# Batch 0's norm sums, the turn of v's second half and the first squares, reordered in the start-up of a fused attention and channel-mix kernel

## The chip, the core and the metric

One NeuronCore of a Trainium2 chip. The metric is the device time of one execution in microseconds (us). The engines are named as in the profile: PE (matmuls), PEld (its weight loads), DVE, ACT, POOL (which issues most input DMAs here) and SP.

## The reference, cut to what matters

```
qn = q / (norm(q over N) + 1e-6);  kn likewise                 # B, N, C = 4, 6208, 256
a  = softmax(kn^T qn)                                          # 256 x 256 for each batch
x  = v @ a                                                     # then the channel mix on x:
xk = mu_k * x + (1 - mu_k) * x_prev;  xr likewise with mu_r    # x_prev: the row before
y  = sigmoid(xr @ w_r) * (relu(xk @ w_k)**2 @ w_v)             # 256 -> 1024 -> 256
```

Batch 0's attention matrix must be complete before anything of the channel mix can start. After that the kernel walks over 48 blocks of 512 rows, with the sums of batches 1 to 3 interleaved.

## The kernel before

Batch 0 comes in groups of 512 rows (`DIRECT = NB - 1 = 11`). Each group is cast to bf16, squared for k's norms, and multiplied by PE. Squares of groups 1 to 10 are added on DVE; those of groups 0, 11, 12 and 13 go through PE as matmuls against a column of ones.

```python
    def group_cast(g, between):          # between: the two DVE steps of the sum of group g-1
        ...
        nc.vector.tensor_copy(row[...], f[0][:rows, :n]...)             # L145
        if g == NB - 1:
            v_mark()                     # a memset; it releases all of POOL's loads
        if between:
            between.pop(0)()             # L167
        mid = row[:rows, :n, P:P + C]
        if g < DIRECT:
            for go in between: go()      # L170, L172
            nc.scalar.copy(mid, f[1][:rows, :n])                        # L155
        else:
            nc.vector.tensor_copy(mid, f[1][:rows, :n])                 # L157
            for go in between: go()
        nc.scalar.activation(k2[:rows, :n], f[1][:rows, :n], AF.Square) # L160
```

After the sums, the softmax of batch 0 and the first block's x:

```python
    vT0 = const.tile([P, 2, M + 1], BF16, name="vT0")     # v of block 0, turned; 2 = halves of C
    ...
        def turn_half(a):      # PE: four 128x128 transposes into half a of ONE PSUM tile (L444)
        def take_half(a, copy):                            # that half to SBUF (L447)
            copy(vT0[:, :, a * H + 1:(a + 1) * H + 1]..., vT_ps[:, 2 * a:2 * a + 2])
        def difference(a):     # DVE: vT0 columns of half a minus the columns one to the left (L479)
        def product(a, ih):    # PE: four matmuls (L487) on vT0[:, ih, half a] and its difference
    ...
    evac_first()               # DVE: S out of PSUM, scaled (L332)
    turn_half(0)
    turn_half(1)
    take_half(1, nc.scalar.copy)
    turn()                     # PE: S transposed (L353)
    keep_warm(2)
    go = v_transpose_pe(1, nc.scalar.copy)                 # block 1's v, turned by PE (L425)
    invert_first(1)
    take_half(0, nc.vector.tensor_copy)
    difference(0)
    exp()                      # ACT (L361)
    go()
    weigh_first(0)             # DVE: a_sb (L373, L374)
    weigh_first(1)
    difference(1)
    for a in range(2):
        for ih in range(2):
            product(a, ih)
        for dh in range(2):
            mix_first("xk", a, dh)                         # DVE (L498)
```

Then `up_first` multiplies xk by w_k (L511), ACT applies Relu (L513, later L576), DVE squares (kk, L584). In the main loop, `square(0, 3)` (the first four kk of block 0) stood ahead of the two `mix` of block 1's xk (L556).

## Time and profile before

| | |
|---|---|
| time, first three runs | 505.04, 505.09, 505.9 us, median 505.09 |
| span of the profiled run | 503.7 us (that run took 505.44) |
| PE busy | 481.4 us, 96% |
| PE busy from 60 us on | 9.98 to 10.00 of every 10 us, but for 0.2 us near 130 and the last stretch |

Read the slices first: PE is full from the fourth slice on, so only the start-up can give anything. The prediction shows those lines and the waits.

### The profile page before, as it was taken

How to read it: one execution, taken by the hardware profiler on the slowest of the kernel's cores; microseconds unless marked ns; L12 is line 12 of the kernel's file. 1: busy time of each engine (PE TensorE's matmuls, PEld its weight loads, DVE VectorE, ACT ScalarE, POOL GpSimd, SP SyncE). 2: the span in 40 equal slices, each digit the busy share in tenths (PEclk: the TensorE clock that was granted, in tenths of full speed). 3: DMA queues.
4: the chain of work that ended last, by engine and by line, in shares of the span. 5: the costliest groups of instructions: out<-in, count | busy, mean ns of one | idle time of the engine just before them, and what ended most of it. 6: DMA issues, size and time to landing. Idle time of an engine off the chain costs nothing.

```text
span 503.7 us, 9289 instructions
## 1 busy us (share of the span) xinstructions
PE 481.4 (96%) x3429; PEld 330.8 (66%) x3429; DVE 429.0 (85%) x789; ACT 428.8 (85%) x872; POOL 97.3 (19%) x143
## 2 busy tenths in 40 slices
PE   1689999999999999999999999999999999999996
PEld 1355677667666666776676676666666666666675
DVE  2778899998988998899889899899888787878784
ACT  4788999899989989888999898988888878788784
POOL 0044332222233222122123322110031010000000
PEclk9999999999999999999999999999999999999999
DMA  8999999999999999996699999982295858343123
GB/s 324 419 311 192 183 143 188 142 183 199 210 216 196 217 177 179 146 208 110 142 195 146 181 184 185 163 145 73 64 208 97 160 88 151 80 103 89 55 72 105
DMA packets 131558, 83.46 MB, mean 166 GB/s; under 512 B 50548, under 2 KB 125624, under 8 KB 130488
## 3 DMA queue, kind: packets, MB, share of 16 engines
q0 software_dynamic: 55840, 33.01, 51.7%
q1 hardware_dynamic: 75352, 49.59, 42.9%
q8 instruction: 27, 0.44, 0.4%
q10 hardware_dynamic: 320, 0.26, 0.2%
q14 instruction: 19, 0.16, 0.1%
HBM read 78.71 MB, written 25.43 MB: 207 GB/s over the span
## 4 chain that ended last, share of the span: by engine, by line
PE 87%; DMA 6%; ACT 3%; DVE 2%; issue 1%; SPq 1%; ACTq 0%; DVEq 0%
PE vr_ps L603 32%; PE kT_ps L571 32%; PE vr_ps L599 8%; PE xT_ps L465 8%; PE s_ps L293 6%; DMA vT<-v_bf 3%; DMA f<-in_k_dram 3%; ACT k L160 1%; ACT qk L155 1%; SPq L125 1%; PE s_ps L199 0%; PE y_ps L643 0%; DVE xk L556 0%; PE st_ps L353 0%; DVE k L167 0%
## 5 line engine op out<-in xcount | busy, mean ns | idle before, releaser
L576 ACT ACTIVATE kr<-kT_ps 128x512 bf16<-128x512 f32 (+1 forms) x390 | 234.5, 604 | 32.9 <-PE kT_ps L571 29.0
L603 PE MATMUL vr_ps<-w_v_sb,kk 128*128 128x256 bf16 x1536 | 230.2, 273 | 0.0
L571 PE MATMUL kT_ps<-xk,w_k_sb 128*128 128x512 bf16 (+1 forms) x780 | 230.0, 377 | 0.2 <-DVE xk L556 0.2
L603 PEld LDWEIGHTS <-kk 128*128 128x128 bf16 x1536 | 150.3, 98 | 57.3
L584 DVE TENSOR_TENSOR kk<-kr 128x2048 bf16<-128x2048 bf16 (+1 forms) x148 | 125.8, 851 | 0.2 <-ACT kr L576 0.2
L613 DVE SCALAR_TENSOR_TENSOR res<-res,vr_ps 128x256 f32<-128x256 f32 x192 | 80.0, 417 | 50.9 <-ACT res L612 50.9
L571 PEld LDWEIGHTS <-w_k_sb 128*128 128x128 bf16 x780 | 75.5, 98 | 27.5 <-issue 0.6
L612 ACT ACTIVATE res<-vr_ps 128x256 f32<-128x256 f32 x192 | 76.5, 399 | 2.3 <-PE vr_ps L603 1.3
L599 PE MATMUL vr_ps<-w_r_sb,xr 128*128 128x256 bf16 x384 | 73.3, 273 | 0.0
L467 ACT CAST xT<-xT_ps 128x512 bf16<-128x512 f32 x94 | 55.9, 594 | 20.0 <-PE xT_ps L465 19.7
L556 DVE SCALAR_TENSOR_TENSOR xr<-delta,mu_t,xT 128x512 bf16<-128x512 bf16 x94 | 70.0, 746 | 0.0
L556 DVE SCALAR_TENSOR_TENSOR xk<-delta,mu_t,xT 128x512 bf16<-128x512 bf16 x94 | 70.0, 746 | 0.0
L599 PEld LDWEIGHTS <-xr 128*128 128x128 bf16 x384 | 37.6, 98 | 44.7 <-issue 0.4
L133 POOL DMA_DIRECT2D qk<-in_q_dram x39 | 26.1, 668 | 159.8 <-ACT kr L576 129.8
L465 PE MATMUL xT_ps<-vT,a_sb 128*128 128x512 bf16 x188 | 55.9, 379 | 0.2 <-DMA vT<-v_bf 0.2
L293 PE MATMUL s_ps<-qk 128*128 128x256 bf16 (+1 forms) x294 | 55.8, 273 | 0.0
L254 ACT ACTIVATE sq<-qk 128x1024 bf16<-128x1024 bf16 x48 | 51.1, 1064 | 0.0
L408 POOL DMA_DIRECT2D v_bf<-in_v_dram x47 | 35.7, 761 | 69.4 <-DMA vT<-v_bf 49.2
L199 PE MATMUL s_ps<-qk 128*128 128x384 bf16 (+2 forms) x98 | 19.1, 340 | 16.6 <-ACT qk L155 16.1
L546 DVE TENSOR_TENSOR delta<-xT 128x1024 bf16<-128x1024 bf16 x47 | 32.3, 686 | 1.1 <-ACT xT L467 1.1
L293 PEld LDWEIGHTS <-qk 128*128 128x128 bf16 (+1 forms) x294 | 28.5, 98 | 5.6 <-issue 0.8
L133 POOL DMA_DIRECT2D qk<-in_k_dram x39 | 25.9, 664 | 5.7 <-DMA v_bf<-in_v_dram 2.5
(114 smaller groups left out, 252.2 us busy)
## 6 DMA issues: line engine op xcount, KB each, us to landing
out_dram<-res SPq DMA_DIRECT2D x47, 512.0 KB, 4.9
v_bf<-in_v_dram POOLq DMA_DIRECT2D x47, 256.0 KB, 8.6
qk<-in_q_dram POOLq DMA_DIRECT2D x36, 256.0 KB, 8.4
qk<-in_k_dram POOLq DMA_DIRECT2D x36, 256.0 KB, 9.4
f<-in_q_dram SPq DMA_DIRECT2D x4, 1024.0 KB, 13.5
f<-in_k_dram SPq DMA_DIRECT2D x4, 1024.0 KB, 11.0
f<-in_q_dram SPq DMA_DIRECT2D x3, 512.0 KB, 7.7
f<-in_k_dram SPq DMA_DIRECT2D x3, 512.0 KB, 6.1
```

Source lines behind the costliest of these rows:

```text
L133: nc.gpsimd.dma_start(rows_at(qk, b, g, i)[:rows, :n], qk_src(t, b, g))
L293: nc.tensor.matmul(s_ps[:, ih, :], rows_at(qk, b, g, 0)[:rows, s, ih * P:(ih + 1) * P], rows_at(qk, b, g, 1)[:rows, s, :], start=t0 and ih ...
L465: nc.tensor.matmul(xT_ps, a_sb[:, b, ih, dh * P:(dh + 1) * P], vT[:, :, ih, :], start=ih == 0, stop=ih == 1)
L467: nc.scalar.copy(xT[:, dh, 1:], xT_ps)
L556: nc.vector.scalar_tensor_tensor(o[:, dh], st[i, "d"][:, dh], mu[:, dh:dh + 1], st[i, "x"][:, dh, :M], op0=OP.mult, op1=OP.add)
L571: nc.tensor.matmul(kT_ps[:, :m], w_k_sb[:, dh, fh * P:(fh + 1) * P], xk[:, dh, :m], start=dh == 0, stop=dh == 1)
L576: nc.scalar.activation(kr, kT_ps[:, :m], AF.Relu, scale=0.5 ** 0.5)
L584: nc.vector.tensor_tensor(st[i, "kk"][:, fh // 4 * 4 + lo:fh + 1, :m], kr, kr, op=OP.mult)
L599: nc.tensor.matmul(vr_ps[:, D:], xr[:, dh, s * P:(s + 1) * P], w_r_sb[:, dh, :], start=dh == 0, stop=dh == 1)
L603: nc.tensor.matmul(vr_ps[:, :D], kk[:, fh, s * P:(s + 1) * P], w_v_sb[:, fh, :], start=fh == 0, stop=fh == 7)
L612: nc.scalar.activation(res[:, s], vr_ps[:, D:], AF.Tanh, scale=0.5)
L613: nc.vector.scalar_tensor_tensor(res[:, s], res[:, s], 1.0, vr_ps[:, :D], op0=OP.add, op1=OP.mult)
```

## The change

Its intent: get batch 0's S to the softmax earlier, take v's half-copy off ACT's path to the exponential, and give PE block 1's xk before kk is squared. Three parts:

```diff
-    DIRECT = NB - 1
+    DIRECT = NB - 2                               # part 1: sums end with group 9
-        if g < DIRECT:
+        if g <= DIRECT:
-        for g in range(DIRECT + 1, LAST + 1):
+        for g in range(DIRECT + 2, LAST + 1):
         if g == DIRECT + 1:
             norms_first()                         # now ahead of group 11's matmuls
+        elif g == DIRECT + 2:
+            norms_of(g - 1)                       # eight more norm matmuls
     turn_half(0)
+    turn()                                        # part 2
     turn_half(1)
-    take_half(1, nc.scalar.copy)
-    turn()
...
     weigh_first(1)
+    take_half(1, nc.vector.tensor_copy)
     difference(1)
...
-            if j > 0 and 0 <= i + 1 < NBLK:
+            if j > 0 and 0 <= i + 1 < NBLK and (i, j) != (-1, 4):
                 square(i + 1, j - 1)              # part 3
...
                     mix(n, "xk", int(j > 4))
+                if (i, j) == (-1, 5):
+                    square(0, 3)
```

## The prediction

> **What bounds the kernel now.** I began with the page's totals and slices, for if TensorE (PE) is full, only stretches where it is not can be shortened.
>
> ```profile
> PE 481.4 (96%) x3429; PEld 330.8 (66%) x3429; DVE 429.0 (85%) x789; ACT 428.8 (85%) x872; POOL 97.3 (19%) x143
> PE   1689999999999999999999999999999999999996
> DMA  8999999999999999996699999982295858343123
> ```
>
> PE is 9 or more from the fourth slice (38 us) on; the busy time of each engine by stretches says how full that is (columns: window, length, then the busy us of PE, PEld, DVE, ACT, POOL):
>
> ```profile
> 20.00:40.00 20.00, 15.22 (x113) 9.06 (x112) 15.27 (x44) 16.67 (x26) 7.61 (x11) 1.00 1.01 320
> 40.00:60.00 20.00, 19.29 (x136) 12.51 (x137) 16.35 (x32) 18.73 (x39) 7.09 (x12) 1.00 1.24 202
> 60.00:70.00 10.00, 10.00 (x72) 6.78 (x71) 8.96 (x16) 9.21 (x20) 3.89 (x7) 1.00 1.39 144
> ```
>
> From about 50 us PE has no hole to remove. The change touches nothing after 50 us, so all it can do is start that stretch earlier; the end then moves by the same amount. What PE waited for in the whole run names the candidates (us in total, times, longest):
>
> ```profile
> PE s_ps L199 <- ACT qk L155: 16.1, 9, 10.1
> PE x_ps L487 <- DVE sm L373: 0.6, 1, 0.6
> PE s_ps L199 <- DVE qk L157: 0.6, 1, 0.6
> PE kT_ps L511 <- ACT kr L513: 0.3, 1, 0.3
> PE kT_ps L571 <- DVE xk L556: 0.2, 1, 0.2
> ```
>
> The 16.1 us is the loading of batch 0, which the change does not touch. The other four add up to 1.7 us: a ceiling of 0.3% of 505.09. The chain of waits (start, us, what) gives their order:
>
> ```profile
> 32.19 0.61 DVE qk L157
> 32.84 1.46 PE s_ps L199 x8
> ...
> 36.71 1.28 ACT L739
> 38.00 0.21 ACT gate L739
> 38.21 0.48 ACT vT L447
> 38.72 0.44 DVE vT L447
> 39.18 0.43 DVE delta L479
> ...
> 45.97 0.69 DVE delta L546
> 46.66 1.14 DVE kk L584
> 47.80 1.34 DVE xk L556 x2
> 49.17 0.38 PE kT_ps L571
> ```
>
> In this reading, group 11's cast (L157) holds S; v's half-copy on ACT holds the copy on DVE; kk stands ahead of the xk that PE needs.
>
> **What the Trainium skill says.**
> - "TensorE: Matmul & The Clock Gate", section "Wait — 56ns, not 53.3ns?": starts of small matmuls are never closer than about 25 ns. The trace agrees: the eight 128x1 norm matmuls start at 34.71 and the next matmul at 34.92, 26 ns each.
> - "ScalarE: Activation LUTs", section "What ACT_TABLE_LOAD costs": about 1283 ns. The load at 36.71 took 1.28 us. The page adds a drain of about 1380 ns; here the next ACT instruction starts at 38.00, so I do not charge it.
> - "PSUM — Partial Sum Buffer", section "PSUM bank collisions raise a hardware error": two engines may not touch one bank and quadrant together, so accesses are guarded by bank. This fits two waits: DVE's copy of v's first half at 38.72 behind ACT's copy of the second half (38.11, 0.57), both out of one bank; and the wait of PE L511 for ACT's Relu of the other half of its bank.
>
> **Part 1: group 10's sum.** Before, DVE halves group 10's squares while casting group 11. The first add (L167) waits for ACT's square to 31.77, and the cast L157 follows at 32.11. Its matmuls (L199 x8) start at 32.84, though the eight before them started at 30.82 and go one per 0.162 us: PE was free at 30.82+8x0.162 = 32.12. So 0.72 us is lost. After, the three DVE adds (0.42, 0.28, 0.42) are gone, the cast follows the memset at 31.69 and ends at about 32.3. PE first runs the norm matmuls, which need only group 9's sum (done 31.1) and group 10's square (31.7): 34.14 to 34.92 before, 0.78 us. So they take 32.12 to 32.90, and the group's matmuls start at 32.90, now behind PE alone. Added are eight norm matmuls for group 11, 0.21 us. Net: 0.78 has moved into the hole, 0.21 is new, and the start goes from 32.84 to 32.90, so the diagonal matmuls (L192, 35.57) come at 32.90+1.30+0.21+0.65 = 35.06: **0.51 us earlier**. The last group's inputs permit it: its k landed by 34.45, its square ends at 35.08, its norms are wanted at 35.53.
>
> **Part 2: v's second half.** The whole softmax chain moves by 0.51. The table load ends at 37.49, rk on DVE at 38.01 (38.52 before), the turned S at about 38.06. Moving the half-copy off ACT lets exp start near 38.1 instead of 38.61, only a little more than the shift itself. But DVE's first half-copy loses its wait: it starts at 38.05, not 38.72; then difference at 38.51, reciprocal 38.84, a_sb 39.03, and PE's product at 39.46 instead of 40.14: 0.68 gained. Block 1's v holds PE until 38.92 (its DMA) and its transposes issue until 39.36, so nearly nothing more was to be had. Turning the half behind S avoids meeting its DMA (PE waited until 37.20 for it, where S now wants to start at 37.23). The price: the half-copy (0.43, 0.46 start to start) now stands on DVE between a_sb and the second difference, which ends at 40.65 (40.87 before). The second product, which had slack there, now waits for it and starts its last matmul at 40.71+6x0.109 = 41.36 instead of 41.80. **0.44 remain.**
>
> **What cuts it.** PE's first up matmul (L511) waited for w_k's DMA:
>
> ```profile
> 41.99 0.10 PEld L511 LDWEIGHTS <-w_k_sb 128*128 128x128 bf16 x1 [0.20 <-DMA w_k_sb<-in_moe_w_k_dram]
> ```
>
> The memset that releases those loads stays at 31.63, so w_k lands at 42.0 as before. xk's first half is ready earlier, and both matmuls run at 42.08 and 42.19 instead of 42.08 and 42.47. Relu comes at 42.49 instead of 42.77, and the matmul behind it at 42.93 instead of 43.21. **About 0.3 of the 0.44 survives**, down to delta of block 1 at 45.67.
>
> **Part 3: kk behind xk.** Nothing is removed on DVE. Before, PE issued its first block-1 matmul at 48.63, would have been ready for the second 0.215 later at 48.85, and got xk at 49.17: 0.32 lost. xk now goes first and is done near 47.7, so **0.32 is added**. kk ends at 45.67+0.61+1.34+1.22 = 48.84; its first reader comes at 50.47-0.62 = 49.85, and the last kk (50.33-0.30 = 50.03) is read from 50.61. ACT's Relu of block 1 rewrites kr's buffer and so waits for kk: it could start at 49.1, after 48.84, so nothing is lost, with 0.2 us to spare.
>
> **Sum.** 0.51 grows to 0.68, falls to 0.44 and 0.30 on DVE and w_k's DMA, and gets 0.32 from the swap: 0.62 us. 505.09-0.62 = 504.5; span 503.7 to 503.1.
>
> **The rivals.**
> 1. The loads absorb part 1 and part 2 altogether: w_k lands some tenths later, or Relu's turn does not move. Then only the swap pays, 0.3 us: 504.8. For it: w_k is a wait of PE already, and the DMA rows are 9 throughout. Against: the loads' issue does not move, and PE was also held after w_k, by xk.
> 2. The swap backfires: kk, 1.34 us later in DVE's order, holds ACT's Relu of block 1, and through the three kT buffers PE. For it: ACT is 18.73 of 20 us busy there, margin 0.2 us. Against: kk's inputs are long ready. Cost up to 0.3: 504.8, and with rival 1 505.1.
> 3. The gain is lost in the long stretch: a transposing DMA issued at 113.25 landed 16.72 us later and held PE for 0.2 us. Other alignments could cost or save some tenths. PE's 10.00 of 10 us speaks against more.
> 4. w_k lands earlier, or xk's second half is later than worked out: the sum reaches 0.76 or 0.5.
>
> **Range and chances.** The mechanisms give 504.3 to 505.1. The three times before are 505.04, 505.09 and 505.9, so a median of a few runs may sit 0.2 off. I take 504.5, from 504.0 to 505.2. A change of 2% would be 10 us; the holes concerned hold 1.7. Faster 0.01, same 0.98, slower 0.01.
>
> **What would show it.** Right: PE's wait on L157 gone and L192 near 35.1; exp near 38.1; DVE's half-copy without a wait behind ACT; PE's product near 39.5, with a new wait of about 0.3 us before the second product; w_k still landing near 42.0; no wait on xk L556 near 48.6; the steady stretch 0.6 us earlier. Wrong: L192 late because group 11's cast or the last loads were the true bound; L511 as late as before (rival 1); ACT's L576 waiting for kk (rival 2); the start earlier but the end not (rival 3).

## The result

| | before | changed |
|---|---|---|
| median of 4 runs | 505.06 (505.03 to 505.9) | 504.73 (504.57 to 504.87) |
| ratio | | 0.9989, 95% interval 0.9972 to 1.0007 |
| span of the profiled run | 503.7 | 503.1 |

A ratio is the mean time of one kernel's runs over the mean of the other's runs of the same rounds, so not quite the ratio of the medians. The time lies in the predicted range, and the span is exactly the predicted 503.1. The steps under that number did not all come true: parts 1 and 3 gave what they were to give, and part 2, worked out as a small loss, took back most of part 1 (0.42 us alone, e2).

The changed kernel's page and its 40 to 60 us stretch (columns as in the prediction):

```profile
PE 482.3 (96%) x3437; PEld 331.2 (66%) x3437; DVE 429.7 (85%) x787; ACT 428.2 (85%) x871; POOL 96.9 (19%) x143
PE   2789999999999999999999999999999999999996
```

```profile
40.00:60.00 20.00, 19.42 (x139) 12.68 (x138) 16.78 (x31) 18.51 (x41) 7.07 (x12) 1.00 1.25 202
```

The eight new norm matmuls are there, and DVE has two instructions fewer (three adds gone, the half-copy come from ACT); of the 20 us, PE is busy 0.13 us more. What PE waited for in the whole run:

```profile
PE s_ps L199 <- ACT qk L155: 14.8, 7, 10.0
PE st_ps L353 <- DVE s_sb L332: 0.8, 1, 0.8
PE x_ps L487 <- DVE a_sb L374: 0.6, 1, 0.6
PE kT_ps L511 <- ACT kr L513: 0.3, 1, 0.3
PE x_ps L487 <- DVE vT L447: 0.2, 1, 0.2
```

Group 11's cast (L157) and block 1's xk (L556) are gone, as predicted. Two waits are new: of S's turn on DVE's s_sb (L353), since S no longer stands behind v's second half, and of the product on DVE's half-copy (vT L447). The chain of waits shows where it stands:

```profile
36.05 0.48 DVE rn L325
...
37.38 0.83 PE st_ps L353 x4
38.20 0.24 PE vT_ps L444 x4
38.47 0.44 DVE vT L447
38.93 0.43 DVE delta L479
...
40.28 0.34 DVE vT L447
40.66 0.50 PE x_ps L487 x3
41.19 0.38 ACT xT L491
```

Two things here are not in the prediction. PE's transposes of v's second half (L444), now behind S, stand ahead of DVE's copy of the *first* half. And the copy of the second half holds the *first* product. PE's instructions in order of time show the second point, in the kernel before and then in the changed one; the fourth and fifth matmul of the first product:

```profile
40.48 0.27 PE L487 MATMUL x_ps<-delta,a_sb 128*128 128x256 bf16 x1
40.59 0.28 PE L487 MATMUL x_ps<-vT,a_sb 128*128 128x256 bf16 x1
```

```profile
40.21 0.27 PE L487 MATMUL x_ps<-delta,a_sb 128*128 128x256 bf16 x1
40.66 0.27 PE L487 MATMUL x_ps<-vT,a_sb 128*128 128x256 bf16 x1 [0.18 <-DVE vT L447]
```

0.11 us from the fourth to the fifth became 0.45. A fair comparison needs a common zero, because group 10's matmuls start by chance at 30.82 in one profile and at 30.68 in the other (when the loads land). So from here positions count from the start of group 10's eight matmuls (L199 x8), the last work that no part touches:

| start, us after group 10 | before | changed |
|---|---|---|
| first product, 1st matmul | 9.32 | 9.19 |
| first product, 5th matmul | 9.77 | 9.98 |
| second product, last matmul | 10.98 | 11.18 |
| L511, the pair that waits for Relu | 12.39 | 12.59 |
| L465, x of block 2 | 18.57 | 18.44 |

At the pair, the changed kernel had *lost* 0.20 us; part 3 then gained 0.33. (0.30 of that loss belongs to neither part 1 nor part 2: one DVE instruction of 256 numbers, L325 at 36.05, took 0.47 us in this profile and 0.17 in the kernel before. The part on why the prediction was right comes back to it.) Of the 0.6 us between the spans, 0.27 were there at 49 us: 0.14 from the earlier group 10, minus 0.20, plus 0.33. The rest arose between 110 and 140 us. Matched by the starts of L465, the shift is 0.27 until 112, 0.44 at 120, 0.82 at 130, and 0.60 to 0.61 from 139 to the end. The kernel before had its 0.22 us wait on a transposing DMA there, which the changed one did not; its profiled run was also 0.38 us slower than its median. That the span came out at the predicted value was chance.

### The profile page after: what moved, and what is told of

Its sections match the earlier page's. It is cut to its first block, busy times and chain, and to the rows that moved or that the text cites. A ratio compares the mean times of both kernels' runs of the same rounds, so it can differ in the third digit from the quotient of the medians.

```text
span 503.1 us, 9303 instructions
## 1 busy us (share of the span) xinstructions
PE 482.3 (96%) x3437; PEld 331.2 (66%) x3437; DVE 429.7 (85%) x787; ACT 428.2 (85%) x871; POOL 96.9 (19%) x143
## 4 chain that ended last, share of the span: by engine, by line
PE 92%; DMA 4%; ACT 2%; DVE 1%; issue 0%; SPq 0%; ACTq 0%; DVEq 0%
PE vr_ps L603 33%; PE kT_ps L571 33%; PE vr_ps L599 8%; PE xT_ps L465 8%; PE s_ps L293 6%; DMA f<-in_k_dram 4%; ACT k L160 1%; PE s_ps L199 1%; ACT qk L155 1%; PE st_ps L353 0%; PE y_ps L643 0%; PE kT_ps L511 0%; PE bank L217 0%; PE vT_ps L425 0%; DVE xk L498 0%
## 5 line engine op out<-in xcount | busy, mean ns | idle before, releaser
L556 DVE SCALAR_TENSOR_TENSOR xr<-delta,mu_t,xT 128x512 bf16<-128x512 bf16 x94 | 70.0, 746 | 0.0
L556 DVE SCALAR_TENSOR_TENSOR xk<-delta,mu_t,xT 128x512 bf16<-128x512 bf16 x94 | 70.0, 745 | 0.0
L465 PE MATMUL xT_ps<-vT,a_sb 128*128 128x512 bf16 x188 | 55.9, 379 | 0.0
L199 PE MATMUL s_ps<-qk 128*128 128x384 bf16 (+2 forms) x98 | 20.2, 357 | 14.8 <-ACT qk L155 14.8
```

The costliest lines, as they stand in the source:

```text
L465: nc.tensor.matmul(xT_ps, a_sb[:, b, ih, dh * P:(dh + 1) * P], vT[:, :, ih, :], start=ih == 0, stop=ih == 1)
L556: nc.vector.scalar_tensor_tensor(o[:, dh], st[i, "d"][:, dh], mu[:, dh:dh + 1], st[i, "x"][:, dh, :M], op0=OP.mult, op1=OP.add)
```

## The experiments

**Theory.** Part 1 gained about 0.5, part 2 gave it back through the two waits named above, and part 3 paid. **Rival.** The loads, w_k's above all, absorb whatever part 1 gains, and part 2 does not matter. Twelve kernels ran, in three groups on one chip each (chip 13, 13 and 8), five rounds and a profile each. All were correct. The table shows all positions (us after group 10) and times; "before" is the kernel before in the same rounds.

| run | 1st product | 5th | last | pair L511 | x of block 2 | time | before | ratio (95%) |
|---|---|---|---|---|---|---|---|---|
| e1, part 1 | 8.77 | 9.23 | 10.44 | 12.85 | 19.00 | 505.37 | 505.45 | 0.9995 (0.9983 to 1.0007) |
| e2, part 2 | 9.41 | 10.20 | 11.40 | 12.81 | 18.99 | 505.68 | 505.45 | 1.0003 (0.9990 to 1.0016) |
| e3, part 3 | 9.94 | 10.40 | 11.61 | 13.02 | 18.88 | 505.37 | 505.45 | 0.9996 (0.9984 to 1.0008) |
| e4, parts 1 and 3 | 9.03 | 9.47 | 10.67 | 12.33 | 18.16 | 504.76 | 505.45 | 0.9987 (0.9974 to 0.9999) |
| e5, changed again | 8.89 | 9.68 | 10.88 | 12.80 | 18.63 | 504.79 | 505.53 | 0.9988 (0.9976 to 1.0000) |
| e6, halves apart | 8.52 | 8.97 | 10.43 | 12.41 | 18.24 | 504.92 | 505.53 | 0.9993 (0.9980 to 1.0005) |
| e7, e4 + w_k split | 8.78 | 9.24 | 10.46 | 11.86 | 18.24 | 505.12 | 505.53 | 0.9994 (0.9982 to 1.0006) |
| e8, e6 + w_k split | 8.65 | 9.09 | 10.38 | 11.84 | 18.14 | 504.55 | 505.53 | 0.9984 (0.9972 to 0.9996) |
| e9, part 1 + w_k split | 9.08 | 9.52 | 10.72 | 12.27 | 18.43 | 504.81 | 505.30 | 0.9986 (0.9968 to 1.0003) |
| e10, before + w_k split | 9.35 | 10.04 | 11.26 | 12.66 | 18.84 | 505.41 | 505.30 | 1.0000 (0.9981 to 1.0018) |
| e11, e8 + v 2 earlier | 8.47 | 9.12 | 10.58 | 11.76 | 17.84 | 504.45 | 505.30 | 0.9982 (0.9964 to 1.0000) |
| e12, e7 + v 2 earlier | 9.04 | 9.72 | 10.94 | 12.34 | 18.20 | 504.58 | 505.30 | 0.9979 (0.9959 to 0.9998) |

The times of one kernel scatter by a microsecond here (before: 504.85 to 506.66, and one 508.23), so the readings rest on the traces, and a difference of 0.2 us in two medians is not evidence.

### e1: part 1 alone

```diff
 # kernel before, with the DIRECT, group_cast, norms_of and norms_last lines of the change only
```

> Part 1 alone (sums a group sooner, norms spread), v's half-copy and the order of kk and xk as in the kernel before. All positions are counted from the start of group 10's eight matmuls (30.82 in the kernel before, 30.68 in the changed one). Kernel before: last matmul of the second product at 10.98, the pair L511 that waits for Relu at 12.39. Changed kernel: 11.18 and 12.59, so parts 1 and 2 together lost 0.2 us there. My theory now: part 1 gained and part 2 gave it back, because the first product waits for the half-copy on DVE and because the first half-copy waits for PE's second half behind S. Then part 1 alone puts the last product matmul at 10.5 to 10.7 and L511 at 12.0 to 12.15, and the time 0.25 to 0.4 us under the kernel before. Rival (the loads absorb part 1): L511 stays within 0.1 of 12.39 with a wait on w_k's DMA, time unchanged.

Measured: the last product matmul at 10.44, 0.54 earlier, which is the part's predicted 0.51. Then PE's weight load stood for w_k:

```profile
42.50 0.44 PEld L511 LDWEIGHTS <-w_k_sb 128*128 128x128 bf16 x5 [1.55 <-DMA w_k_sb<-in_moe_w_k_dram]
```

w_k landed 8.5 us after its issue, against 7.6 in the kernel before, and the pair came 0.46 *later* than before. So my theory is right on the product, the rival is right that w_k takes the gain away (though it had put the pair within 0.1 of 12.39), and the time did not move.

### e2: part 2 alone

```diff
     turn_half(0)
+    turn()
     turn_half(1)
-    take_half(1, nc.scalar.copy)
-    turn()
@@
     weigh_first(1)
+    take_half(1, nc.vector.tensor_copy)
```

> Part 2 alone (v's second half turned behind S and copied by DVE). My theory: exp does not move by more than 0.1, the first half-copy on DVE starts no earlier than before because it waits for PE's second half, the fifth matmul of the first product waits for the second half-copy on DVE, and the last product matmul comes 0.2 to 0.4 later (11.2 to 11.4 after group 10 instead of 10.98); time 0.2 to 0.4 us over the kernel before. Rival (part 2 is a gain and part 1 was the one that failed): the last product matmul at 10.8 or earlier, time under the kernel before.

Measured: the last product matmul 0.42 later. DVE's first half-copy started at 38.83 against 38.72 before, now behind PE's second half. ACT's exponential gained nothing from the missing copy: it started at 38.60 against 38.61, held by PE's turned S. The fifth matmul waited as in the changed kernel:

```profile
41.02 0.27 PE L487 MATMUL x_ps<-vT,a_sb 128*128 128x256 bf16 x1 [0.18 <-DVE vT L447]
```

Part 2 as written is a loss in the trace, 0.42 us at this point; the time is 0.23 us higher, inside the scatter.

### e3: part 3 alone

```diff
-            if j > 0 and 0 <= i + 1 < NBLK:
+            if j > 0 and 0 <= i + 1 < NBLK and (i, j) != (-1, 4):
                 square(i + 1, j - 1)
@@
+                if (i, j) == (-1, 5):
+                    square(0, 3)
```

> Part 3 alone (first kk of block 0 behind xk of block 1). Both theories: nothing moves before 45 us, PE's wait of 0.17 us on xk L556 goes, x_half of block 2 (L465) comes 0.27 to 0.32 earlier (18.57 after group 10 before, 18.25 to 18.30 now), time 0.3 us under the kernel before. If ACT's Relu were held by kk, an idle stretch of ACT ahead of L576 near 49 would show and the gain be under 0.15.

Measured: x of block 2 at 18.88, so the position missed, because in this run the second half of block 0's v landed late:

```profile
38.14 0.40 PE L444 MATMUL vT_ps<-ident,v_bf 128*128 128x128 bf16 x4 [1.19 <-DMA v_bf<-in_v_dram]
```

But the stretch that the part concerns is clean. From the pair to x of block 2 it is 6.15 to 6.18 us in the kernel before, e1, e2, e9 and e10, and 5.83 to 5.86 in the changed kernel, e3, e4, e5, e6 and e12. The swap is worth 0.32 to 0.33 us, and the wait on xk L556 is gone wherever it is in: in the kernel before, PE's fourth matmul of this row came alone at 49.17 (in the prediction's chain); in e3 the four go together.

```profile
48.67 1.03 PE L571 MATMUL kT_ps<-xk,w_k_sb 128*128 128x512 bf16 x4
```

(e7, e8 and e11 have the swap too, but their stretch holds other waits, named there.) In time it shows as 0.08 us, inside the scatter.

### e4: the changed kernel without part 2

```diff
 # the changed kernel, with turn_half, take_half and turn where the kernel before has them
```

> The changed kernel without part 2. My theory: the gains of e1 and e3 add up: last product matmul 10.5 to 10.7 after group 10, x_half of block 2 at 17.9 to 18.05, time 0.5 to 0.7 us under the kernel before (near 504.45), so 0.2 to 0.35 under the changed kernel's 504.73. Rival (loads absorb part 1): the same as the changed kernel, 504.7 to 504.8, L511 at 12.4.

Measured: last product matmul at 10.67 (in the expected band), x of block 2 at 18.16 (0.11 over it), time 0.69 under the kernel before (in the band). The product did not wait for DVE. It was held by the DMA of block 1's v (0.6 us at L425), and L511 again by w_k (0.8 us at its weight load). Against the changed kernel of the first job the trace is 0.28 us better at x of block 2. In time the changed kernel did as well in its own second job (e5), so the times do not tell the two apart.

### e5: the changed kernel again

> The changed kernel once more, on the chip of the next three, as their yardstick. Both theories: 0.1 to 0.4 us under the kernel before. In the trace the fifth matmul of the first product again waits for DVE's half-copy (0.45 us after the fourth), and the first half-copy waits for PE's second half. w_k's landing was 7.0 us after its issue in the first profile of this kernel and 7.6 to 8.4 in others; if it lands after 42.1 here, PE's L511 waits for it, and how late the product was no longer matters (rival 1 of the prediction).

Measured: here group 10's norms were inverted without the slow instruction of the first profile (L325 took 0.17, not 0.47), so the last product matmul came at 10.88, 0.10 *before* the kernel before's. It repeats both waits, the first longer (DVE's instructions in order of time; in the kernel before, this copy waited 0.20 for ACT's):

```profile
38.12 0.43 DVE L447 COPY vT<-vT_ps 128x512 bf16<-128x512 bf16 x1 [0.48 <-PE vT_ps L444]
```

and then w_k took 8.4 us to land:

```profile
42.57 0.61 PE L511 MATMUL kT_ps<-xk,w_k_sb 128*128 128x256 bf16 x4 [0.78 <-DMA w_k_sb<-in_moe_w_k_dram]
```

So in the changed kernel either wait can be the last: the product in the first profile (w_k in 7.0 us), w_k in this one. The position of the pair (12.80) is no better than before, yet the time is 0.74 lower than the kernel before of the same rounds. The one profile of the kernel before had an early w_k (7.6 us; 8.1 to 8.5 in e1 to e6), so it is probably a lucky yardstick for this stretch.

### e6: v's halves apart

```diff
-    vT0 = const.tile([P, 2, M + 1], BF16, name="vT0")
+    vT0 = const.tile([P, 2, 2, M // 2 + 1], BF16, name="vT0")   # half, half of C, column
 # the two halves' turns in two PSUM tiles: one tagged kT_ps, one s_ps
     exp()
+    nc.scalar.copy(vT0[:, 1, :, 0:1], vT0[:, 0, :, H:H + 1])    # the doubled column
     go()
```

> The changed kernel with v's two halves in separate regions of their SBUF tile (one column doubled, copied by ACT) and their turns in two PSUM banks, so that neither the first half-copy has to wait for PE's second half nor the first product for the second half-copy. If these two waits are what part 2 cost: no wait on L447 before the fifth matmul, which starts 0.11 to 0.3 after the fourth; first product matmul 8.9 to 9.0 after group 10's start (9.19 in the changed kernel), last one 10.8 to 10.9 (11.18). The time then depends on w_k: if it lands before 41.5, 0.2 to 0.3 us under the changed kernel; if later, the same as the changed kernel. If the waits had another cause, the fifth matmul still waits.

Measured: both waits are gone, and the fifth matmul follows the fourth at 0.12 us:

```profile
39.70 0.27 PE L488 MATMUL x_ps<-delta,a_sb 128*128 128x256 bf16 x1
39.82 0.28 PE L488 MATMUL x_ps<-vT,a_sb 128*128 128x256 bf16 x1
```

DVE's two copies in e6, the first without a wait:

```profile
37.81 0.41 DVE L448 COPY vT<-vT_ps 128x512 bf16<-128x512 bf16 x1
39.68 0.42 DVE L448 COPY vT<-vT_ps 128x512 bf16<-128x512 bf16 x1
```

The fifth matmul (39.82) runs while the second copy runs (39.68 to 40.10), and the result is correct. First product at 8.52 and last at 10.43: 0.37 and 0.45 us earlier than in e5, more than I had expected (8.9 and 10.8). So what part 2 cost were those two waits, and they came from what shares a tile, not from data. In `vT0`, the first half's columns of the second C half lie, in address, between the two pieces that the second half-copy writes. The matmul that reads them waited for that copy, and with the halves in separate regions it does not. That the span of addresses decides is inferred; it fits the first and third matmul, whose v columns lie outside that span and which did not wait. DVE's first copy waited for PE's second half, whose results go to the same PSUM tile; with two tiles it does not. (The two tiles also lie in buffers of 2 KB a partition each, a bank's size, so e6 does not tell tile from bank.) What is left is the wait that the prediction had worked out, of the second product on its difference: 0.34 us from its first matmul (40.27) to its second.

```profile
40.61 0.28 PE L488 MATMUL x_ps<-delta,a_sb 128*128 128x256 bf16 x1
```

Nothing came of the repair in time (504.92), and w_k held PE again (1.1 us at its weight load).

### e7 and e8: w_k in two pieces

```diff
-    nc.gpsimd.dma_start(w_k_sb, moe_w_k.rearrange("(ko ki) f -> ki ko f", ki=P))
+    for c in (slice(0, C), slice(C, DF)):
+        nc.gpsimd.dma_start(w_k_sb[:, :, c], moe_w_k.rearrange("(ko ki) f -> ki ko f", ki=P)[:, :, c])
```

e7 is e4 with this, e8 is e6 with this.

> e4 (changed kernel without part 2) with w_k loaded in two pieces, the 256 columns that the first two matmuls need first. If w_k's landing absorbs part 1: PE's wait on w_k is gone, the first L511 starts right after the first xk, the pair behind Relu at 11.8 to 12.1 after group 10's start (12.33 in e4, 12.85 in e1), time 0.2 to 0.4 us under e4's distance to the kernel before (0.7), so 0.9 to 1.1 under the kernel before. Rival (the extra DMA pushes the later loads, block 2's v and w_v, into PE's way): new waits on DMA between 46 and 51 us and no gain over e4.

> e6 with the split load of w_k. If both repairs do what I claim: last product matmul 10.8 to 10.9 after group 10's start, the pair L511 at 12.2 to 12.3, time 0.1 to 0.2 us over e7 and 0.3 to 0.5 under the changed kernel. If part 2 as such costs (the copy on DVE instead of on an idle ACT), e8 stays over e7; if only the two waits cost, the two are equal.

Measured: no wait on w_k in either, and the pair at 11.86 and 11.84 (e4: 12.33, e6: 12.41). The gain of part 1 now arrives there: 0.53 and 0.55 us before the kernel before. The repaired part 2 is level with no part 2 at all (I had expected e8's pair at 12.2 to 12.3). But the rival for e7 came true as well. POOL issues one load more, and block 2's v lands too late (e7):

```profile
46.40 0.59 PE L571 MATMUL kT_ps<-xk,w_k_sb 128*128 128x512 bf16 x2
47.35 0.62 PE L425 MATMUL vT_ps<-ident,v_bf 128*128 128x128 bf16 x8 [0.36 <-DMA v_bf<-in_v_dram]
```

What remains at x of block 2 is 18.24 and 18.14. PE's wait for that v is 0.36 us in e7 and 0.29 in e8. In time e8 is 0.98 under the kernel before, e7 only 0.41, where I had expected 0.9 to 1.1.

### e9 and e10: the split alone, and with part 1

e9 is e1, e10 the kernel before, each with the split load.

> Part 1 alone with w_k in two pieces. If w_k's landing is what absorbed part 1 in e1: PE's wait on w_k gone, the pair L511 at 11.8 to 12.0 after group 10's start (12.85 in e1, 12.39 in the kernel before), wait on xk L556 (0.17) still there, time 0.3 to 0.6 us under the kernel before, against 0.1 for e1. If part 1 were lost elsewhere: the pair stays at 12.4 or later.

> The kernel before with w_k in two pieces, to see what the split is worth by itself. The pair L511 there was held by xk, not by w_k, so it should stay at 12.3 to 12.45 after group 10's start and the time within 0.2 us of the kernel before. If the split itself is the gain (w_k was the bound all along): the pair at 12.0 or earlier and the time 0.3 us or more lower.

Measured: e9's pair at 12.27, not the 11.8 to 12.0 I had expected. The wait on w_k is gone (PE's first weight load of L511 stands at 41.56, without a wait), but here block 1's v held PE for 1.0 us ahead of the product. Against e1 it is still 0.58 earlier, and the time is 0.49 under the kernel before (e1: 0.08). e10's pair stays behind the kernel before's (12.66, over the expected 12.3 to 12.45) and its time does not move (505.41 against 505.30): the split shows no gain by itself. This run had two delays of its own: block 1's v held PE for 0.7 us, and DVE's second a_sb (L374) took 0.64 us instead of 0.35, so that here too the fifth matmul came 0.36 after the fourth, with no half-copy in the way. So in e1, w_k's landing is what swallowed part 1; e10 shows no gain from the split where part 1 is missing.

### e11 and e12: block 2's v ahead of w_r

```diff
-    nc.gpsimd.dma_start(w_r_sb, ...)
     v_load(2)
+    nc.gpsimd.dma_start(w_r_sb, ...)
```

e11 is e8 with this, e12 is e7 with this.

> e8 with block 2's v loaded before w_r instead of after it. The wait of 0.29 us on that v near 47 us, which the split load had brought, should go: the first matmul of x of block 2 (L466) at 17.75 to 17.9 after group 10's start (18.14 in e8, 18.44 in the changed kernel, 18.57 before), no new wait on w_r, which is read only near 49.6; time 0.1 to 0.3 us under e8's distance to the kernel before (1.0). If the DMA rings as a whole are late, v's wait stays and nothing is gained.

> e7 with block 2's v loaded before w_r. As e11: the wait of 0.36 us on that v goes, x of block 2 (L465) at 17.8 to 17.95 after group 10's start (18.24 in e7). With e11 it compares part 2, repaired, with no part 2 at all: I expect the two within 0.15 us of each other in the trace and not to be told apart in time.

Measured, e11: v's wait is gone (from the 47 us stretch; after batch 0 has landed, PE's matmuls show no wait on any DMA in the start-up), x of block 2 at 17.84, 0.73 us before the kernel before. It could have come 0.2 sooner: from the pair it takes 6.08 us, for the pair's second matmul waited for xk's second half (the fifth matmul of the product came 0.31 after the fourth, as L374 took 0.54). The time, 0.85 under the kernel before, falls short of what I had expected (0.1 to 0.3 better than e8's 0.98).

```profile
46.70 0.61 PE L425 MATMUL vT_ps<-ident,v_bf 128*128 128x128 bf16 x8
```

e12: the same wait is gone, but x of block 2 comes at 18.20, outside the band. Without part 2, PE meets v's second half ahead of S, and it landed late again; block 1's v then held PE for 0.7 us ahead of the product, and L374 took 0.58. So the two kernels, expected within 0.15 us of each other, lie 0.36 apart here:

```profile
37.16 0.40 PE L444 MATMUL vT_ps<-ident,v_bf 128*128 128x128 bf16 x4 [0.57 <-DMA v_bf<-in_v_dram]
```

In the six runs with v's second half behind S (the changed kernel, e2, e5, e6, e8, e11) PE never waited for it. Of the eight with it ahead of S, it did in five: e1 (0.17), e3 (1.19), e9 (0.27), e10 (0.31) and e12 (0.57). So part 2's order of the turns looks like an insurance against this landing; its sharing of tiles was its price. The medians of e11 and e12 (504.45 and 504.58) are the lowest here beside e8's 504.55. e11 is 0.85 and e12 0.72 us under the kernel before of their rounds. The changed kernel was 0.33 and 0.74 under the kernel before of its two jobs (504.73 and 504.79). Its second distance is as good as e12's and near e11's, so none of these repairs is shown to be faster than the changed kernel.

## Why the prediction was right, and where it was not

The time fell in the range, 0.23 over the centre, but partly by luck, for two of the steps below failed. The mechanism that bounds the result (only the start of the full stretch can move, and the end moves by the same amount) held up to 112 us: the shift stayed at 0.27 us, where the prediction had 0.6. The rest of the span's 0.6 came later (point 6). Taken by its steps:

1. **Part 1, "0.51 us earlier": right.** L192 lies 4.22 after group 10 in the changed kernel (34.90 - 30.68) and 4.75 before (35.57 - 30.82): 0.53. Alone (e1) it carried through to the last product matmul as 0.54.
2. **Part 2, "0.44 remain": wrong, and this is the step that failed.** The prediction let DVE's first half-copy "lose its wait" and let only the second product wait for the second half-copy. In the runs, the first half-copy got a new wait (on PE's second half, 0.30 and 0.48 us), and the first product waited for the second half-copy. Of the 0.5 that part 1 brings, 0.10 was left at the last product matmul in e5, and -0.20 in the first profile. Alone part 2 cost 0.42 (e2); with both waits removed it cost nothing (e6: 10.43 against e1's 10.44). (The first profile's -0.20 also has the 0.30 of the slow L325: 0.53 - 0.43 - 0.30.) I had counted durations and data, and not what a semaphore is placed for when two pieces share a tile. For PSUM the prediction even names the guard by bank, in its third point on the skill, and reads DVE's old wait by it; it did not apply it to PE's turns, which it had itself moved behind S, into the bank that DVE reads. With the sharing removed, its sum for part 2 holds: it put the first product at 8.64 after group 10 (39.46) and the last matmul at 10.54 (41.36), and e6 has 8.52 and 10.43.
3. **"About 0.3 survives": wrong.** Nothing survived at the pair (12.59 and 12.80 against 12.39). In the first profile that was point 2 and the slow L325, for w_k came early. In e5 and e1 it was rival 1 of the prediction, w_k. I had argued that w_k lands at 42.0 as before; its time to land was 7.0 to 8.5 us over the eight runs with the whole load, which one profile could not tell me.
4. **Part 3, "0.32 is added": right**, 0.32 to 0.33 between all runs without another wait in that stretch. Relu of block 1 shows no wait on kk: rival 2 did not happen.
5. **Sum, 0.62.** By the first profile, the steps made 0.13 at x of block 2 (18.57 to 18.44); by the medians 0.33, and 0.74 in the second job. The yardstick was probably lucky, as e5 suggests, so the true gain cannot be read from one pair of traces. It is less than a microsecond and not told from zero by the intervals of the first job.
6. **Rival 3** (other alignments in the long stretch) is what turned 0.27 us at 49 us into a span shorter by 0.6. The prediction's list of waits leaves out, without a mark, the line that belongs to it, `PE xT_ps L465 <- DMA vT<-v_bf: 0.2, 1, 0.2`; with it the ceiling is 1.9 us, not 1.7.

What stays open: why L325, 256 numbers on DVE, took 0.47 us in the first profile of the changed kernel and in e4, and 0.17 elsewhere. (Its second instance took 0.31 to 0.34 in the kernel before, the changed kernel, e2, e3 and e4, and 0.16 elsewhere.) "SBUF — State Buffer", section "SBUF: two separate sides", names a candidate: DVE's faster modes and POOL exclude each other on one port pair, and POOL was issuing loads then. The traces fit it. The slow L325 ends with POOL's issue (changed kernel):

```profile
35.77 0.76 POOL L733 DMA_DIRECT2D w_r_sb<-in_moe_w_r_dram  x1
36.05 0.47 DVE L325 TENSOR_SCALAR rn<-rn 128x2 f32<-128x2 f32 x1 [0.19 <-ACT rn L322]
```

In e5 it starts earlier in the same issue (0.14 us after its start, not 0.28) and takes 0.17. All seven slow instances of L325 end within 0.01 us of the end of such an issue. Every fast one in the fourteen traces either started within 0.23 us of an issue's start or would not have ended before the issue anyway. But no run moved the issues, so this is a fit and not a proof. Open, too, is why the loads' time to land varies by up to 1.5 us from run to run.

## What to carry to other kernels

Before you move a copy behind other work, list what its tile shares: here a later write into the same PSUM tile, and a region whose addresses enclose those of another piece, each brought a wait that no data flow explains, and two PSUM tiles and separate regions removed them. In a start-up that is a string of loads, a gain on compute arrives only as far as the next landing, so read each load's landing over several runs before you count on one of them. And give all positions from a common event that the change does not touch, or the scatter of the loads passes for an effect.

## What the Trainium skill lacked or had wrong

- "PSUM — Partial Sum Buffer": it advises to read another bank than the one that matmuls write, but gives no figure for what sharing a bank costs. A copy of one half of a bank waited 0.30 to 0.48 us for transposes into the other half, and separate PSUM tiles removed the wait (first product 0.37 us earlier, e5 to e6).
- No page has the counterpart in SBUF: a matmul waited (0.45 us from the fourth to the fifth instead of 0.12) for a copy into columns that it does not read, while the addresses that the copy spans enclose its own. In e6 the same matmul ran while that copy ran, so the data do not ask for the wait; that it comes from the placing of semaphores is inferred.
- "ScalarE: Activation LUTs": the drain of about 1380 ns after a table load does not appear here; the next ACT instruction starts 1.29 us after the load's start in both kernels (36.71 to 38.00, 36.04 to 37.33), and the load itself starts 0.01 us after the instruction before it ends (36.70, 36.03).
- "SBUF — State Buffer" does not say in which part of a DMA issue POOL holds the ports that it shares with DVE. If they are what held L325, it was a late part: of issues of 0.5 to 1 us, those met within 0.23 us of their start did not hold it (0.16 to 0.17 us), and the seven held instances (0.31 to 0.47 us) had met theirs 0.28 to 0.62 us after its start.
- "DMA: Bandwidth & Descriptors" gives typical bandwidths and latencies, but no spread of landing times under load: the same 512 KB load landed 7.0 to 8.5 us after its issue in eight runs, and this decided whether part 1's gain reached the pair (7.0: no wait on w_k; 8.4 and 8.5: PE held, e5 and e1).
